# A Conformer block on one core: the fourth value product's left-over keys on all 128 rows, the last softmax sums in two bf16 halves, and the second batch's value loads three ticks apart

## The chip, the cores and the metric

The kernel runs on one core of a Trainium2 chip. The metric is the device time of one execution in microseconds; of the kernel before there are three timed runs and one profiled execution. The core has five engines with queues of their own: TensorE (PE, with its weight loads listed apart as PEld), VectorE (DVE), ScalarE (ACT), GpSimd (POOL) and SyncE (SP), which here issues nearly all transfers.

## What is computed

One Conformer block on `x` of 2 x 4000 x 512 in bf16 (D = 512, F = 2048). Cut to what matters here:

```
h  = layernorm(x);  x1 = x + 0.5 * (silu(h @ w_ff1_a) @ w_ff1_b)
h  = layernorm(x1); q, k, v = h @ w_q, h @ w_k, h @ w_v
p  = softmax(q @ k^T * D**-0.5)            # over 4000 keys, per batch
x2 = x1 + (p @ v) @ w_o
h  = layernorm(x2); a, b = split(h @ w_pw1)
dc = depthwise_conv(a * sigmoid(b), 3 taps); dc = batchnorm(dc)
x3 = x2 + silu(dc) @ w_pw2
h  = layernorm(x3); x4 = x3 + 0.5 * (silu(h @ w_ff2_a) @ w_ff2_b)
out = layernorm(x4)
```

## The kernel before, in words

**Tiling.** Tokens go in 16 chunks of up to 512 (`NCK`, eight a batch, `TCB`); the last chunk of a batch has 416. The 4000 keys of a batch make `KT` = 32 tiles of 128 rows: 31 full ones and a left-over tile with `REST` = 32 keys. Stages follow each other: first feed-forward over all chunks, attention over all chunks with the convolution of earlier chunks beside it, the rest of the convolution, second feed-forward.

**Attention.** `attention` walks over chunks `g` and, in each, over 32 ticks `kt`. Big products are done two by two blocks at a time with seven products in place of eight: keys in pairs of tiles (15 pairs), the 512 columns of the values in halves of `HD` = 256, the queries in halves of `hw` (256 columns, or 208 in the short chunk). `pv(g, n, pairs)` issues value product `n` of the seven for some pairs, each as two 128x`hw` matmuls on 128 rows of keys. Pairs come in groups `j` = 0 to 7 (`group`: pair 0, then pairs 2j-1 and 2j); `units` issues products 1, 3, 7, 5, 6 of group `j` from tick 4j+3 on. What is left of chunk `g-1` is issued in the first ticks of chunk `g` by `units_late`: `late_first`, `late_second` (with the left-over keys for products 7, 3 and 2), and `late_third` in ticks 2 to 6 (products 2 and 4 of all 15 pairs, then the left-over keys for product 4).

**Left-over keys.** Tile 30 (128 keys) and tile 31 (32 keys) have no partner and are done plainly by `pv_rest(g, tail, ns)`. For tile 31 (`tail` = 1) the probabilities lie four times in `ptail`, once in each group of 32 rows, and the 32 keys lie four times in `h[31]`; each product number in `ns` takes a row group of its own with `tile_position`. Products 7, 3 and 2 are issued together, in three row groups; product 4 alone, two matmuls on rows 0 to 31. Its values are `Vs[1]`, the difference of the two halves of `h[31]`, made by `v_rest(1)` on DVE: for batch 1 in tick 27 of chunk 0 (steps in `keys_swap`), for batch 2 in chunk 8.

**Softmax sums.** One column of the value halves is ones, so the sum of the probabilities comes out as one row of a product. `sum_row` puts it into `lrow`, one row of 512 f32 numbers. In chunks 0 to 14 it goes through memory into a column per query. After the last chunk, `attention_end` calls `sums_direct` between `late_third` for product 2 and `late_third` for product 4: four f32 matmuls of one row by one column (`lrow` times 1.0) turn the row into four columns, and a reciprocal gives `rl`. The projections of the last chunk read `rl` when they add to the residual.

**Values of batch 2.** While batch 1 is worked on, `v_ahead` makes the forms of batch 2's values and stores them. In chunk 8 `v_back(j, 0)` loads group `j` of the halves (`hv`, 256 KB a pair) and `v_back(j, 1)` the fourth form `V4`. All are issued by SP. `v_stream` loads the two other forms (`V12`, from `v12d`) per group and chunk; `key_queries` loads keys transposed.

**Order.** The calls are not the order of issue. `Plan` takes all instructions with estimated costs, keeps PE close to the order of the calls (it may issue ready work up to 8 us of estimated time early), and orders the other engines by due time. It makes six passes and takes the best by its own estimate. `Plan.cost` counts a matmul with `tile_position` at a quarter. Waits between engines are on semaphores; each engine works in its order.

All instructions pass through one helper, so the profile gives them one line; groups are told apart by the tiles: `y` and `s` are the PSUM banks, `sums`, `xt`, `keys`, `work` and `wff` the five regions of SBUF.

Of the kernel before, what the change touches and what calls it, by code (L numbers as in the profile page):

```python
# [8 lines left out]
ALU = mybir.AluOpType  # L9
# [3 lines left out]
B, T, D, F, KW = 2, 4000, 512, 2048, 3  # L13


TILE = 128
TPC = 4
CHUNK = TPC * TILE
# [11 lines left out]
HC, HD, HF = CHUNK // 2, D // 2, FC // 2  # L30
KT = -(-T // 128)
REST = T % 128
# [9 lines left out]
def width(c):  # L42

    return CHUNK if c % TCB < TCB - 1 else T - (TCB - 1) * CHUNK
# [515 lines left out]
class Conformer:  # L560
# [35 lines left out]
    def memory(self):  # L596
# [32 lines left out]
        o = oF + 2 * 6 * 2 * HC  # L629
# [16 lines left out]
        o = TCB * 4096  # L646
# [7 lines left out]
        at = [8192 + t % self.CONV_SLOTS * 4096 if t < self.NBESIDE else 20480 + (t - self.NBESIDE) * 4096  # L654
              for t in range(NCK)]
# [20 lines left out]
        C = Region(nc, "work", 48992)  # L676
        off = [0]

        def take(n):
            o = off[0]  # L680
            off[0] += n
            return o
# [18 lines left out]
        oHL = take(2048)  # L701
# [36 lines left out]
        self.zero, self.b_zero = self.P[0], self.b_P[0]  # L738
        lrow, self.b_lrow = C.view(oACC + 2048, CHUNK, F32, parts=1), C.buf("lrow", oACC + 2048, 4 * CHUNK)
        self.lrow, self.lflat = lrow.rearrange("o (p t) -> o t p", t=TPC), lrow  # L740
        self.lrowd = nc.dram_tensor("lrowd", [1, CHUNK], F32, kind="Internal").ap()
        self.b_lrowd = Buf("lrowd")
        self.u4, self.b_u4 = C.view(oACC, CHUNK, F32), C.buf("u4", oACC, 4 * CHUNK)
# [1122 lines left out]
    def pv_rest(self, g, tail, ns):  # L1866

        W, hw = width(g), width(g) // 2
        kt = KT - 1 if tail else KT - 2
        x, b_x = (self.ptail, self.b_ptail) if tail else (self.P30, self.b_P30)  # L1870
        v, b_v = self.h[kt], self.b_h[kt]
        vs, b_vs = self.Vs[tail], self.b_Vs[tail]
        forms = {3: (v[:, HD:D], b_v, 0), 7: (v[:, HD:D], b_v, 1), 2: (v[:, 0:HD], b_v, 0), 4: (vs, b_vs, 1)}
        for u in range(2):
            for j, n in enumerate(ns):
                form, b, q = forms[n]
                ps, b_ps = self.bank(self.PV_BANK[n])
                r, at = (slice(j * REST, (j + 1) * REST), {"tile_position": (j * REST, 0)}) if tail else (slice(0, 128), {})
                self.mm(ps[:, u * hw:(u + 1) * hw], form[r, u * 128:(u + 1) * 128], x[r, q * hw:(q + 1) * hw],
                        False, u == 1, [b, b_x], b_ps, skip_group_check=True, **at)  # L1880

# [56 lines left out]
                  self.v12d[b][i:i + n].rearrange("n p d -> p n d"), self.b_V12[j % 2][at:at + n], reads=self.b_v12d[b][i:i + n])  # L1938

    def v_rest(self, k):  # L1940
        x = self.h[KT - 2 + k]
        self.S.op("DVE", lambda e: e.tensor_tensor(out=self.Vs[k], in0=x[:, 0:HD], in1=x[:, HD:D], op=ALU.subtract),
                  reads=[self.b_h[KT - 2 + k]], writes=[self.b_Vs[k]])

    def v_ahead(self, i, step):
# [263 lines left out]
    def keys_swap(self, g, kt):  # L2209

        at = g * KT + kt
        if g == 0:
            steps = [(1, n) for n in range(5)] if kt == 3 else []
            j, r = divmod(kt + 1, 4)
            if 1 < j < GROUPS:
                steps += {0: [(j, 0)], 1: [(j, 1)], 2: [(j, 3)], 3: [(j, 2), (j, 4)]}[r]
            for j, n in steps:
                self.v_here(j, n)
            if kt in (26, 27):
                self.v_rest(kt - 26)  # L2220
        i, r = divmod(at - KT - 4, 10)
        if 0 <= i < PAIRS:
            for n in {0: (0,), 4: (1, 2), 5: (3, 4), 8: (5,)}.get(r, ()):
                self.v_ahead(i, n)
        if TCB - 1 <= g <= TCB:
            at -= (TCB - 1) * KT
            for k in range(KT):
                if (6 + k * (2 * KT - 12) // KT if k < KT - 1 else KT + 6) == at:
                    self.key_queries(1, k)
            for j in range(GROUPS):  # L2230
                if at == KT + 3 + j:
                    self.v_back(j, 0)
                if at == KT + 14 + j:
                    self.v_back(j, 1)
            if at in (KT + 11, KT + 12):
                self.key_values(1, KT - 2 + at - KT - 11)
            if at in (KT + 18, KT + 19):
                self.v_rest(at - KT - 18)
# [106 lines left out]
        self.residual(ps, b_ps, tile_at(g, ti), self.rl[s][r, ti:ti + 1], [self.b_rl[s]], r, total)  # L2345

    def sums_direct(self, s):
        ps, b_ps = self.sbank()
        for ti in range(TPC):
            self.mm(ps[0:TILE, ti:ti + 1], self.lrow[:, ti], self.onef[0:1], True, True,  # L2350
                    [self.b_lrow, self.b_onef], b_ps, inc=ti == TPC - 1)
        self.S.op("DVE", lambda e: e.reciprocal(self.rl[s], ps[0:TILE, 0:TPC]),
                  reads=[b_ps], writes=[self.b_rl[s]])

# [799 lines left out]
```

## Time and profile before

| what | value |
|---|---|
| median of 3 runs | 1866.38 us (1866.32 to 1868.34) |
| the profiled execution itself | 1868.96 us |
| its span, first to last instruction | 1864.0 us |
| PE busy | 1845.8 us, 99% of the span |
| DVE, ACT, POOL busy | 77%, 72%, 8% |
| granted TensorE clock, mean | 0.999 |
| moved by DMA | 228.49 MB, mean 123 GB/s |

The span is what the profile shows; the execution's own time has some 5 us more around it. Matmuls are pipelined: the next one starts before the one ahead has ended, so the time from start to start says what one costs, not its duration. In the timeline a row stands for several equal instructions: its first start, its length, their count.

### The profile page before, as it was taken

How to read it: one execution, taken by the hardware profiler on the slowest of the kernel's cores; microseconds unless marked ns; L12 is line 12 of the kernel's file. 1: busy time of each engine (PE TensorE's matmuls, PEld its weight loads, DVE VectorE, ACT ScalarE, POOL GpSimd, SP SyncE). 2: the span in 40 equal slices, each digit the busy share in tenths (PEclk: the TensorE clock that was granted, in tenths of full speed). 3: DMA queues.
4: the chain of work that ended last, by engine and by line, in shares of the span. 5: the costliest groups of instructions: out<-in, count | busy, mean ns of one | idle time of the engine just before them, and what ended most of it. 6: DMA issues, size and time to landing. Idle time of an engine off the chain costs nothing.

```text
span 1864.0 us, 39949 instructions
## 1 busy us (share of the span) xinstructions
PE 1845.8 (99%) x15838; PEld 1488.5 (80%) x15838; DVE 1428.7 (77%) x3087; ACT 1350.1 (72%) x2390; POOL 139.9 (8%) x354
## 2 busy tenths in 40 slices
PE   9999999999999999999999999999999999999998
PEld 6888888866778777887678788778875888888887
DVE  8889999868566767766765667766768888888896
ACT  6887777754656777677666767777768778778776
POOL 3000000000000000000100000000011000000000
PEclk9999999999999999999999999999999999999999
DMA  7333344297545655457944434543475222221211
GB/s 200 84 90 88 82 112 99 64 260 221 168 130 139 180 153 153 118 157 154 250 133 126 125 107 115 139 128 105 120 212 162 63 69 70 67 59 47 60 36 57
DMA packets 312520, 228.49 MB, mean 123 GB/s; under 512 B 191154, under 2 KB 283125, under 8 KB 312068
## 3 DMA queue, kind: packets, MB, share of 16 engines
q1 hardware_dynamic: 311796, 225.59, 44.9%
q8 instruction: 126, 2.06, 0.5%
q14 instruction: 70, 0.57, 0.1%
q10 hardware_dynamic: 528, 0.26, 0.0%
HBM read 128.99 MB, written 55.82 MB: 99 GB/s over the span
## 4 chain that ended last, share of the span: by engine, by line
PE 95%; DVE 2%; DMA 1%; ACT 1%; issue 0%; SPq 0%; POOL 0%; DVEq 0%; ACTq 0%
PE y L95 50%; PE s L95 45%; DVE work L95 1%; ACT work L95 0%; DMA work<-work 0%; DMA wff<-in_w_ff_a_dram 0%; DVE sums L95 0%; DMA xt<-v12d 0%; DVE xt L95 0%; DVE keys L95 0%; ACT keys L95 0%; ACT sums L95 0%; SPq L95 0%; DVE wff L95 0%; DVE s L95 0%
## 5 line engine op out<-in xcount | busy, mean ns | idle before, releaser
L95 ACT ACTIVATE sums<-s 128x512 bf16<-128x512 f32 (+4 forms) x505 | 295.3, 585 | 154.3 <-PE s L95 151.3
L95 DVE TENSOR_TENSOR sums<-sums 128x512 bf16<-128x512 bf16 (+3 forms) x528 | 202.2, 399 | 81.8 <-ACT sums L95 70.5
L95 ACT ACTIVATE keys<-s 128x512 bf16<-128x512 f32 (+3 forms) x275 | 157.0, 574 | 134.4 <-PE s L95 111.3
L95 PE MATMUL y<-work,keys 128*128 128x256 bf16 x1920 | 244.4, 273 | 0.6 <-DVE work L95 0.6
L95 PE MATMUL s<-work,keys 128*128 128x256 bf16 (+5 forms) x1456 | 225.1, 292 | 0.2 <-ACT sums L95 0.2
L95 PE MATMUL s<-sums 128*128 128x256 bf16 (+1 forms) x1428 | 212.5, 272 | 0.8 <-DVE sums L95 0.4
L95 ACT ACTIVATE work<-xt,work 128x512 bf16<-128x512 bf16 x268 | 205.2, 785 | 9.1 <-DVE work L95 7.4
L95 PE MATMUL y<-wff,keys 128*128 128x256 bf16 (+3 forms) x1592 | 209.3, 276 | 0.2 <-DVE keys L95 0.2
L95 PEld LDWEIGHTS y<-work,keys 128*128 128x128 bf16 x1920 | 187.6, 98 | 23.6 <-DVE work L95 1.2
L95 PE MATMUL y<-sums,keys 128*128 128x256 bf16 (+1 forms) x1440 | 205.3, 270 | 0.0
L95 PE MATMUL y<-work,wff 128*128 128x256 bf16 (+3 forms) x1308 | 195.2, 272 | 0.9 <-ACT keys L95 0.8
L95 DVE TENSOR_TENSOR keys<-keys 128x1024 bf16<-128x1024 bf16 (+2 forms) x262 | 170.4, 664 | 25.7 <-ACT keys L95 17.9
L95 PEld LDWEIGHTS y<-wff,keys 128*128 128x128 bf16 (+1 forms) x1592 | 151.2, 98 | 30.3 <-issue 3.3
L95 DVE BATCH_NORM_STATS2 work<-xt 128x6 f32<-128x512 bf16 x251 | 163.1, 682 | 2.5 <-DMA xt<-in_x_dram 1.8
L95 PEld LDWEIGHTS y<-sums,keys 128*128 128x128 bf16 x1440 | 137.9, 98 | 27.5 <-issue 3.5
L95 PEld LDWEIGHTS s<-work,keys 128*128 128x128 bf16 (+1 forms) x1456 | 118.5, 97 | 49.5 <-issue 2.5
L95 PEld LDWEIGHTS s<-sums 128*128 128x128 bf16 x1428 | 138.9, 98 | 23.4 <-DVE sums L95 0.7
L95 POOL TENSOR_TENSOR work<-work 128x4 f32<-128x4 f32 (+3 forms) x107 | 91.1, 854 | 769.2 <-DVE work L95 756.7
L95 PE MATMUL y<-sums,xt 128*128 128x256 bf16 (+1 forms) x960 | 145.2, 270 | 1.2 <-DMA xt<-v12d 1.1
L95 PEld LDWEIGHTS y<-work,wff 128*128 128x128 bf16 x1308 | 126.0, 98 | 18.4 <-issue 1.5
L95 PE MATMUL s<-work 128*128 128x512 bf16 (+4 forms) x545 | 131.6, 375 | 2.0 <-DVE work L95 1.7
L95 PE MATMUL s<-xt,keys 128*128 128x256 bf16 (+1 forms) x816 | 124.1, 270 | 0.0
(153 smaller groups left out, 3176.3 us busy)
## 6 DMA issues: line engine op xcount, KB each, us to landing
xt<-kfd SPq DMA_DIRECT2D x98, 384.0 KB, 3.3
xt<-v12d SPq DMA_DIRECT2D x105, 256.0 KB, 3.0
xd<-xt SPq DMA_DIRECT2D x28, 512.0 KB, 3.9
xt<-xd SPq DMA_DIRECT2D x28, 512.0 KB, 4.8
out_dram<-xt SPq DMA_DIRECT2D x14, 512.0 KB, 2.9
xt<-in_x_dram SPq DMA_DIRECT2D x13, 512.0 KB, 4.4
dcvd<-wff SPq DMA_DIRECT2D x48, 128.0 KB, 3.0
keys<-dcvd SPq DMA_DIRECT2D x12, 512.0 KB, 3.9
```

Source lines behind the costliest of these rows:

```text
L95: return getattr(eng, self.name)(*self.args, **self.kw)
```

## The change

- `pv_rest`: product 4 of tile 31 uses all 128 rows instead of rows 0 to 31. So that rows 32 to 127 add nothing, `Vs[1]` is set to zero once (POOL, tick 25 of chunk 0), and `v_rest(1)` writes rows 0 to 31 alone.
- `sums_direct`: the row of sums is split on DVE into a bf16 part and the bf16 of what is left; eight bf16 matmuls (two a column, added in PSUM) take the place of the four f32 ones.
- `keys_swap`: `v_back(j, 0)` for `j` of 2 and more is issued at ticks 6, 9, 12, 15, 18 and 21 of chunk 8 instead of 5 to 10.

```diff
+        self.lsplit = [C.view(oHL + n * 1024, CHUNK, parts=1).rearrange("o (t p) -> o t p", t=TPC) for n in range(2)]
+        self.b_lsplit = [C.buf("lsplit", oHL + n * 1024, 2 * CHUNK) for n in range(2)]
...
-                r, at = (slice(j * REST, (j + 1) * REST), {"tile_position": (j * REST, 0)}) if tail else (slice(0, 128), {})
+                r, at = (slice(j * REST, (j + 1) * REST), {"tile_position": (j * REST, 0)}) if tail and n != 4 else (slice(0, 128), {})
...
     def v_rest(self, k):
-        x = self.h[KT - 2 + k]
-        self.S.op("DVE", lambda e: e.tensor_tensor(out=self.Vs[k], in0=x[:, 0:HD], in1=x[:, HD:D], op=ALU.subtract),
+        x, r = self.h[KT - 2 + k], slice(0, REST if k else 128)
+        self.S.op("DVE", lambda e: e.tensor_tensor(out=self.Vs[k][r], in0=x[r, 0:HD], in1=x[r, HD:D], op=ALU.subtract),
...
+            if kt == 25:
+                self.S.op("POOL", lambda e: e.memset(self.Vs[1], 0.0), writes=[self.b_Vs[1]])
...
-                if at == KT + 3 + j:
+                if at == KT + 3 + (j if j < 2 else 3 * (j - 1)):
                     self.v_back(j, 0)
...
     def sums_direct(self, s):
+        (hi, lo), (b_hi, b_lo) = self.lsplit, self.b_lsplit
+        self.S.op("DVE", lambda e: e.tensor_copy(hi, self.lrow), reads=[self.b_lrow], writes=[b_hi])
+        self.S.op("DVE", lambda e: e.tensor_tensor(out=lo, in0=self.lrow, in1=hi, op=ALU.subtract),
+                  reads=[self.b_lrow, b_hi], writes=[b_lo])
         ps, b_ps = self.sbank()
         for ti in range(TPC):
-            self.mm(ps[0:TILE, ti:ti + 1], self.lrow[:, ti], self.onef[0:1], True, True,
-                    [self.b_lrow, self.b_onef], b_ps, inc=ti == TPC - 1)
+            for x, b in ((hi, b_hi), (lo, b_lo)):
+                self.mm(ps[0:TILE, ti:ti + 1], x[:, ti], self.one3[0:1, 0:1], x is hi, x is lo, [b, self.b_one3], b_ps,
+                        inc=ti == TPC - 1 and x is lo)
```

## The prediction

> **What bounds the kernel now.** I read the page first, then the stretches by chunk, then the waits of TensorE, then the timeline of each place that the change touches.
>
> ```profile
> span 1864.0 us, 39949 instructions
> PE 1845.8 (99%) x15838; PEld 1488.5 (80%) x15838; DVE 1428.7 (77%) x3087; ACT 1350.1 (72%) x2390; POOL 139.9 (8%) x354
> PE 95%; DVE 2%; DMA 1%; ACT 1%; issue 0%; SPq 0%; POOL 0%; DVEq 0%; ACTq 0%
> ```
>
> TensorE is busy 99% of the span and carries 95% of the chain that ended last. So time is won in two ways only: TensorE issues less or issues closer together, or one of its few waits goes. Work on the other engines and transfers cost nothing until TensorE waits for them. By chunk (the stretches: us, busy us of PE, PEld, DVE, ACT, POOL, granted clock, DMA share, GB/s), chunk 7 and then chunk 8, in which the moved loads are:
>
> ```profile
> 828.00:884.00 56.00, 54.81 (x532) 46.09 (x530) 37.41 (x88) 42.48 (x86) 3.15 (x13) 1.00 0.74 157
> 884.00:952.00 68.00, 67.80 (x499) 44.28 (x497) 46.60 (x117) 44.00 (x79) 5.59 (x21) 1.00 0.90 227
> ```
>
> All that TensorE waits for from the end of chunk 0 to the end of attention (461 to 1376 us; total, times, longest):
>
> ```profile
> PE y L95 <- DMA xt<-v12d: 1.1, 1, 1.1
> PE s L95 <- ACT sums L95: 1.0, 2, 0.8
> PE s L95 <- ACT s L95: 0.3, 1, 0.3
> PE s L95 <- DVE xt L95: 0.2, 1, 0.2
> ```
>
> These 2.6 us in 915 are all that a new order of the other engines can give back there. The busy time hides something else: products on 32 rows.
>
> **Fourth value product (pv_rest, late_third).** One chunk's left-over keys in the timeline of PE (start, us, what):
>
> ```profile
> 475.76 0.38 PE L95 MATMUL y<-sums,work 128*128 128x256 bf16 x2
> 475.98 0.38 PE L95 MATMUL y<-xt,sums 128*128 128x256 bf16 x2
> 476.30 0.39 PE L95 MATMUL y<-wff,sums 32*128 32x256 bf16 x2
> 476.62 0.39 PE L95 MATMUL y<-sums,keys 128*128 128x256 bf16 x2
> ```
>
> Two products on 128 rows take 0.22 us from start to start (475.76 to 475.98). Going into the pair on 32 rows takes 0.32 (475.98 to 476.30), coming out of it 0.32 again: 0.10 lost on each side, 0.20 a chunk. The products themselves are no shorter for having 32 rows: 273 ns each in the group below. On 128 rows the pair is like its neighbours and both losses go. The group (count, busy us, mean ns of one) has all of these pairs, two products a chunk in 14 chunks of 256 columns:
>
> ```profile
> L95 PE MATMUL y<-wff,sums 32*128 32x256 bf16 x28 | 5.4, 273 | 0.0
> ```
>
> In the two short chunks (208 columns) the last one, with the sums ahead of it, reads:
>
> ```profile
> 1376.24 2.85 PE L95 MATMUL y<-sums,keys 128*128 128x208 bf16 x30
> 1379.06 2.02 PE L95 MATMUL s<-work 1*128 1x1 f32 x8
> 1381.01 2.85 PE L95 MATMUL y<-sums,work 128*128 128x208 bf16 x30
> 1383.70 0.34 PE L95 MATMUL y<-xt,sums 128*128 128x208 bf16 x2
> 1383.97 0.35 PE L95 MATMUL y<-wff,sums 32*128 32x208 bf16 x2
> 1384.25 1.90 PE L95 MATMUL s<-work,wff 128*128 128x512 bf16 x8
> ```
>
> Thirty products from 1381.01 to 1383.70 are 0.090 each, 0.18 a pair; the steps around the 32-row pair are 0.27 and 0.28, so 0.19 is lost. Sum: 16 x 0.20 = **3.2 us gained**. The six 32-row products of 7, 3 and 2 keep their mode change. Bounds: 3.0 to 3.2, since in the built order of the changed kernel all 16 pairs stand between 128-row products.
>
> The Trainium skill, page TensorEngine Tiling (Array Packing), section Theoretical Speedup, speaks against this edit: a contraction of 32 or less should run up to four times as fast in tiles. Here two products in one tile have no neighbour tile to run beside, and the rows above decide against the rule; its result is a rival below.
>
> What the edit adds beside: one memset of 128x256 on POOL, once in chunk 0, and a subtraction on 32 rows in place of 128. POOL is busy 8%, and this row is the nearest:
>
> ```profile
> L95 POOL MEMSET work<- 1x512 f32 x1 | 0.5, 514 | 3.3 <-DVE xt L95 3.3
> ```
>
> It stands two ticks ahead of the subtraction that writes after it, so half a microsecond hides there: 0 (if that cover were gone, at most its 0.5).
>
> **Last softmax sums (sums_direct).** Four f32 products run as eight passes. The thirty before them end their issue at 1376.24 + 30 x 0.090 = 1378.93; the next product starts at 1381.01: 2.08 us for the sums. For the eight bf16 products of one row the nearest is the transpose of the taps, four products of three rows:
>
> ```profile
> 61.59 0.82 PE L95 MATMUL y<-work,keys 128*128 128x256 bf16 x6
> 62.34 0.25 PE L95 MATMUL y<-work 3*128 3x3 bf16 x4
> 62.52 0.50 PE L95 MATMUL s<-sums 128*128 128x256 bf16 x3
> ```
>
> Six products of 0.109 end their issue at 62.24, and the next wide one starts at 62.52: 0.28 for four with the change of mode both ways. Four more at some 0.03 make 0.40. So 2.08 - 0.40 = 1.7 is gained on TensorE. Against it stand two DVE operations that the products now wait for, a cast and a subtraction over 512 elements of one row. DVE at this place, and the nearest prices by form:
>
> ```profile
> 1378.30 0.70 DVE L95 TENSOR_TENSOR work<-s,work 1x128 f32<-1x128 f32 x2
> 1381.12 0.18 DVE L95 RECIPROCAL work<-s 128x4 f32<-128x4 f32 x1 [1.84 <-PE s L95]
> 1387.12 1.54 DVE L95 SCALAR_TENSOR_TENSOR xt<-s,work,xt 128x512 bf16<-128x512 f32 x2 [0.66 <-PE s L95]
> L95 DVE CAST xt<-s 128x512 bf16<-128x512 f32 x2 | 1.3, 668 | 0.0
> L95 DVE TENSOR_TENSOR work<-y,sums 128x512 f32<-128x512 f32 x14 | 9.6, 689 | 0.5 <-DVE sums L95 0.2
> ```
>
> The last row sum ends at 1379.00; cast and subtraction, one needing the other, end near 1379.00 + 0.67 + 0.69 + 0.1 = 1380.5. In the built order 14 of the 30 following products now stand ahead of the sums: TensorE gets there at 1378.93 + 14 x 0.090 = 1380.19 and waits some 0.3. Behind the waiting product are 16 products of the same chunk and all projections. I take 1.7 - 0.4 = **1.3 us gained**; 1.7 without a wait, 0.7 if the two operations take half as long again. The reciprocal that follows has 6 us of cover: its first reader starts at 1387.12. The Trainium skill, page VectorE: DVE Perf Modes, section The perf-mode tier table, puts an f32 copy within SBUF at twice the rate of one from PSUM, which my cast row is; by that this term would be 1.6. No row here shows it, and the source is read with a stride.
>
> **Value loads of batch 2 (v_back).** Groups 2 to 7 load at ticks 6, 9, ... 21 of chunk 8 in place of 5, 6, ... 10. Before, on SP:
>
> ```profile
> 888.07 1.57 SPq L95 DMA_DIRECT2D keys<-vhd  x3
> 894.09 6.72 SPq L95 DMA_TRANSPOSE work<-keysd  x1
> keys<-vhd SPq DMA_DIRECT2D x7, 512.0 KB, 5.8
> ```
>
> Chunk 8 is where DMA is busiest (0.90), but TensorE is busy 67.80 of 68.00 there, so spreading has 0.2 us to win. It costs nothing either while the loads come in time: a tick is 68.0/32 = 2.1 us, group j is first used at tick 4j+3, so group 2 still has 5 ticks, 10.6 us, against 5.8 to land; later groups have more. **0**, from -0.2 to 0.3.
>
> **The new order.** The planner reorders everything from chunk 1 to the end of attention. The one DMA wait of chunk 7 is a value form that left SP late:
>
> ```profile
> 857.56 0.32 SPq L95 DMA_DIRECT2D xd<-xt  x1
> 865.24 0.58 SPq L95 DMA_DIRECT2D xt<-v12d  x1
> 867.10 1.26 SPq L95 DMA_TRANSPOSE work<-work  x1
> 869.03 1.20 SPq L95 DMA_TRANSPOSE work<-work  x1
> 870.27 0.58 SPq L95 DMA_DIRECT2D xt<-v12d  x1
> 875.94 0.44 PE L95 MATMUL y<-sums,xt 128*128 128x208 bf16 x3 [1.09 <-DMA xt<-v12d]
> ```
>
> Counted from the same `xd<-xt`, the changed order puts that load ahead of these two transposes and behind one more store, about 2 us sooner: the 1.1 us wait should go (0 to 1.1). Against it ACT has two new runs of four tap scalings ahead of score copies. The known run of four in chunk 15 stays:
>
> ```profile
> 1357.62 2.92 ACT L95 ACTIVATE work<-xt,work 128x512 bf16<-128x512 bf16 x4
> ```
>
> It ends in the 0.8 and 0.3 us waits for ACT above; runs of three, six of them, cost next to nothing. For the two new ones I take 0.3 each, between 0 and 1.1. Net **0.5 us gained**, between 1.1 gained and 2.2 lost.
>
> **Sum.** 3.2 + 1.3 + 0 + 0.5 = 5.0 us. The profiled execution itself took 1868.96 us, so its like would take 1863.96; it ran 2.58 above the median of the runs, 1866.38, from which the forecast is 1866.38 - 5.0 = **1861.4**.
>
> **Rivals.**
> - Only the mode changes count: the sums wait for DVE as long as they save, or the new runs on ACT eat the rest. For it: the sum clears 0.2% (3.7 us, about what a measurement of this kernel can tell from no change) by 1.3 only, and 3.2 alone doesn't. Against it: 1.7 us less issue at the end has few ways to be eaten whole. 1866.38 - 3.2 = 1863.2, the same within 0.2%.
> - Slower: the value loads of chunk 8 come late. Group 2's margin is 10.6 - 5.8 = 4.8 us, and SP is held 6.72 us by one transpose at 894.09. From 5 us of delay on, each microsecond more is an idle one on TensorE, in up to six groups; at 1.5 each, 9 us, 1866.38 + 9 - 4.5 = 1870.9. Against it: the built order puts the loads of groups 0 to 3 ahead of that transpose, and the others have over 12 us.
> - The tile rule: a 32-row pair costs a quarter, 0.05 us, and the change adds 0.17 a chunk, 2.7 in all: 1866.38 + 2.7 - 1.8 = 1867.3, the same. Against it: every 32-row row above.
>
> **How the numbers follow.** The forecast has a chance of 0.68, the first rival 0.25, the slow one 0.05, the tile rule 0.02. The range: best case 3.2 + 1.7 + 1.1 + 0.2 = 6.2, and a microsecond for a median of few runs (they span 2.0), gives 1859.2; at the other end 3.0 + 0.7 - 2.2 = 1.5, 1864.9, which holds the first rival. Faster 0.68, same 0.27, slower 0.05.
>
> **What would show it.** In the changed profile: no `y<-wff,sums` on 32 rows, and steps of 0.22 or 0.18 where they were; the sums in less than 0.8 us, wait included; no wait for `xt<-v12d` in chunk 7; none for `keys<-vhd` in chunk 8; waits for ACT between 461 and 1376 us below 2 us. I am wrong if the steps around the fourth product stay at 0.32, or if new waits of over 2 us stand in that stretch.

## The result, and the profile after

| kernel | median of its runs | lowest to highest | profiled execution, its span |
|---|---|---|---|
| before (6 runs beside the changed one) | 1867.45 us | 1866.32 to 1868.68 | 1868.96 us, 1864.0 |
| changed (6 runs) | 1860.28 us | 1859.74 to 1861.06 | 1859.74 us, 1854.8 |

The ratio is 0.9962 with a 95% interval from 0.9949 to 0.9975: 7 us faster, where 5.0 was forecast (1861.4, from 1859.2 to 1864.9). The page of the changed kernel, its span, the busy time of each engine and the shares of the chain that ended last:

```profile
span 1854.8 us, 39946 instructions
PE 1840.5 (99%) x15838; PEld 1490.4 (80%) x15838; DVE 1429.7 (77%) x3090; ACT 1349.4 (73%) x2388; POOL 140.5 (8%) x356
PE 96%; DVE 2%; ACT 1%; DMA 0%; issue 0%; SPq 0%; DVEq 0%
```

TensorE's count has not moved, since eight bf16 products stand for eight f32 passes. Its busy time fell by 5.3 us, and the DMA's 1% of the chain is gone. The stretches of chunks 7 and 8, cut where each chunk's first product on row groups starts (columns as in the prediction):

```profile
826.59:880.80 54.21, 54.21 (x531) 46.46 (x530) 34.86 (x81) 41.18 (x83) 3.46 (x13) 1.00 0.70 152
880.80:948.69 67.89, 67.69 (x498) 44.44 (x498) 47.51 (x121) 44.37 (x80) 4.30 (x21) 1.00 0.89 233
```

Chunk 7 has no idle time left (54.21 busy of 54.21; before, 54.81 of 56.00). Chunk 8 has what it had. All that TensorE waits for from 461 to 1376 us:

```profile
PE s L95 <- ACT sums L95: 0.9, 2, 0.7
PE s L95 <- DVE work L95: 0.4, 1, 0.4
PE s L95 <- ACT s L95: 0.3, 1, 0.3
```

The `xt<-v12d` wait and the one for DVE's `xt` are gone, a wait for DVE's `work` (the split of the sums) has come. No row names `keys<-vhd`. The left-over keys of the same chunk as before:

```profile
475.27 0.38 PE L95 MATMUL y<-xt,sums 128*128 128x256 bf16 x2
475.49 0.38 PE L95 MATMUL y<-wff,sums 128*128 128x256 bf16 x2
475.71 0.38 PE L95 MATMUL y<-sums,keys 128*128 128x256 bf16 x2
475.93 0.38 PE L95 MATMUL s<-sums,keys 128*128 128x256 bf16 x2
```

Every pair starts 0.22 us after the one ahead; the 0.32 on both sides of the 32-row pair are gone. And the sums, PE first, then DVE:

```profile
1372.80 1.41 PE L95 MATMUL y<-sums,work 128*128 128x208 bf16 x14
1374.15 0.17 PE L95 MATMUL s<-work 1*128 1x1 bf16 x1
1374.69 0.32 PE L95 MATMUL s<-work 1*128 1x1 bf16 x7 [0.37 <-DVE work L95]
1374.95 1.60 PE L95 MATMUL y<-sums,work 128*128 128x208 bf16 x16
```

```profile
1372.17 0.71 DVE L95 TENSOR_TENSOR work<-s,work 1x128 f32<-1x128 f32 x2
1372.91 0.62 DVE L95 CAST work<-work 1x512 bf16<-1x512 f32 x1
1373.57 1.07 DVE L95 TENSOR_TENSOR work<-work 1x512 bf16<-1x512 f32 x1
1375.05 0.18 DVE L95 RECIPROCAL work<-s 128x4 f32<-128x4 f32 x1
```

Fourteen products of 0.0893 end their issue at 1374.05; the next wide one starts at 1374.95. So the sums cost 0.9 us in place of 2.08, 0.37 of it a wait for the subtraction. The first product, on the high half, did not wait for it.

To place the rest, the traces of all kernels but e9, which has no such row groups, are cut at the same products: chunks 1 to 15, then from the last chunk's first product on row groups to the first projection (the sums lie here), then to the third group of 160 columns in the last chunk's product with `w_pw1`. All in us:

| kernel | chunks 1 to 15 | end of attention | projections, to the last `w_pw1` product | span |
|---|---|---|---|---|
| before | 914.68 | 8.29 | 16.40 | 1864.0 |
| before again (e4) | 914.46 | 8.29 | 16.40 | 1861.4 |
| rows, old order (e2) | 911.15 | 8.10 | 16.39 | 1859.9 |
| order alone (e3) | 912.37 | 8.29 | 15.85 | 1861.4 |
| rows and order (e1) | 909.29 | 8.10 | 15.91 | 1857.3 |
| sums alone (e5) | 914.08 | 7.10 | 16.40 | 1861.2 |
| loads alone (e6) | 914.47 | 8.29 | 16.40 | 1864.1 |
| all but the loads (e7) | 910.40 | 6.91 | 15.91 | 1856.7 |
| changed | 909.27 | 6.91 | 15.91 | 1854.8 |
| changed again (e8) | 909.25 | 6.89 | 15.91 | 1855.7 |
| changed, third time (e11) | 909.29 | 6.88 | 15.91 | 1855.6 |
| changed, sums later (e10) | 909.28 | 6.38 | 15.85 | 1855.2 |

From before to changed these three columns lose 5.41 + 1.38 + 0.49 = 7.3 us (7.1 from the second execution of before), which is the whole change of the medians. Some of the 0.49 does not last: to the four 128x128 products at 1415.17 us before and 1407.38 after, counted from the first projection, it is 30.92 against 30.64, so 0.28. What the span varies beyond the three columns (1854.8 against 1855.7 for one program) lies ahead of chunk 1 and behind them, and comes and goes with the execution. Single chunks repeat to 0.02 us from one execution of a program to the next, but for chunks 7 and 8 of those kernels that wait for a transfer there. That is why differences far below the scatter of the whole time can be read here.

### The profile page after: what moved, and what is told of

The parts are those of the page before. It is cut to its first block, busy times and chain, and to the rows that moved or that the text cites. A ratio compares the mean times of both kernels' runs of the same rounds, so it can differ in the third digit from the quotient of the medians.

```text
span 1854.8 us, 39946 instructions
## 1 busy us (share of the span) xinstructions
PE 1840.5 (99%) x15838; PEld 1490.4 (80%) x15838; DVE 1429.7 (77%) x3090; ACT 1349.4 (73%) x2388; POOL 140.5 (8%) x356
## 4 chain that ended last, share of the span: by engine, by line
PE 96%; DVE 2%; ACT 1%; DMA 0%; issue 0%; SPq 0%; DVEq 0%
PE y L95 50%; PE s L95 46%; DVE work L95 1%; ACT work L95 1%; ACT keys L95 0%; DMA xt<-in_x_dram 0%; DMA work<-work 0%; ACT sums L95 0%; DVE wff L95 0%; ACT wff L95 0%; DVE xt L95 0%; DVE sums L95 0%; DVE keys L95 0%; DVE s L95 0%; ACT s L95 0%
## 5 line engine op out<-in xcount | busy, mean ns | idle before, releaser
L95 DVE TENSOR_TENSOR s<-s,xt 128x512 f32<-128x512 f32 (+1 forms) x98 | 67.6, 690 | 94.7 <-PE s L95 65.3
```

The lines of the kernel that those rows point to most:

```text
L95: return getattr(eng, self.name)(*self.args, **self.kw)
```

## The experiments

My theory was that of the prediction: mode changes, then sums, then the planner's order, and nothing for the loads. The rivals: only the mode changes count; the order does it; the loads do it. Dots in the code stand for lines that are not shown. Edits e1 to e6 are shown against the kernel before, e7, e9 and e10 against the changed one. The median of before was 1866.83 us beside e1 to e4 (33 runs), 1867.53 beside e5 to e8 (26 runs) and 1867.04 beside e9 to e11 (15 runs).

**e1: the fourth value product alone.**

```diff
-                r, at = (slice(j * REST, (j + 1) * REST), {"tile_position": (j * REST, 0)}) if tail else (slice(0, 128), {})
+                r, at = (slice(j * REST, (j + 1) * REST), {"tile_position": (j * REST, 0)}) if tail and n != 4 else (slice(0, 128), {})
...
+            if kt == 25:
+                self.S.op("POOL", lambda e: e.memset(self.Vs[1], 0.0), writes=[self.b_Vs[1]])
```

> The fourth product on 128 rows alone; sums and value loads as before. Its order of issue on all engines is that of the changed kernel up to chunk 8. Theory (mode and order): the mode change of the array gives 16 x 0.20 = 3.2 us, and the new order that the planner made of it gives about 2 more (the wait for a value form in chunk 7, 1.1 to 1.6, and small ones): 5.2 to 5.5 below before, no wait for xt<-v12d in chunk 7. Rival (mode alone, the rest of the change gave the rest): 3.2 below.

Measured: 1863.46 us, ratio 0.9983 (0.9974 to 0.9992). By its time that is 3.4 below before, as the rival had it, and not 5.2 to 5.5. In the stretches of its trace it gains more than the 3.3 us of mode changes: 5.39 + 0.19 + 0.49 = 6.1 against before; why the time shows less comes under e3 and e8. The chunks are those of the changed kernel, and TensorE's order of issue is the same but for the sums. So this edit, and not the sums or the loads, carries the new order: the planner counts a matmul with `tile_position` at a quarter, and the pair now has its full cost.

**e2: the same edit, but the planner goes on costing the pair at a quarter,** so that its order stays the old one.

```diff
-            return (n / 2.4 + 2.5) * (0.25 if at is not None else 1)
+            return (n / 2.4 + 2.5) * (0.25 if at is not None or self.quarter else 1)
...
+                if self.S.plan:
+                    self.S.plan.quarter = bool(tail and n == 4)
```

> The fourth product on 128 rows, but the planner still counts the pair at a quarter, so that the order of issue on every engine stays that of before. Mode and order: 3.2 us below before, steps of 0.22 us around the pair in all chunks, and the wait for xt<-v12d of about 1.1 us stays in chunk 7. Rival (the time is won by the 128-row pair itself, wait included): 5 below, and the wait is gone.

Measured: 1864.59 us, 0.9986 (0.9977 to 0.9995), so 2.2 below before, between 0.9 and 4.3; the trace tells more. Its rows at the left-over keys, and what TensorE waits for from 461 to 1376 us:

```profile
475.32 0.38 PE L95 MATMUL y<-xt,sums 128*128 128x256 bf16 x2
475.54 0.38 PE L95 MATMUL y<-wff,sums 128*128 128x256 bf16 x2
475.76 0.38 PE L95 MATMUL y<-sums,keys 128*128 128x256 bf16 x2
```

```profile
PE s L95 <- ACT sums L95: 1.0, 2, 0.8
PE y L95 <- DMA xt<-v12d: 0.6, 1, 0.6
PE s L95 <- ACT s L95: 0.3, 1, 0.3
PE s L95 <- DVE xt L95: 0.2, 1, 0.2
```

Steps of 0.22, with all the old waits in place: the mode changes by themselves.

**e3: the order alone.** The pair stays on 32 rows, and the planner is told its full cost.

```diff
-            return (n / 2.4 + 2.5) * (0.25 if at is not None else 1)
+            return (n / 2.4 + 2.5) * (0.25 if at is not None and not self.full else 1)
...
+                if self.S.plan:
+                    self.S.plan.full = bool(tail and n == 4)
```

> The fourth product stays on 32 rows, but the planner counts the pair in full: the order of issue is that of e1, the mode change is kept. Mode and order: 1.6 to 2.3 us below before, no wait in chunk 7, steps of 0.32 us around the pair. Rival (mode alone): the same as before within 0.5. Rival (tile rule): as the rule has the pair at a quarter, e1 is slower than this one by 2.7.

Measured: 1866.38 us, 0.9997 (0.9988 to 1.0006), the same by its time, as the first rival had it. In the stretches, though, it gains 2.1 in the chunks and 0.55 behind them against e4. Its steps and waits:

```profile
475.42 0.38 PE L95 MATMUL y<-xt,sums 128*128 128x256 bf16 x2
475.73 0.39 PE L95 MATMUL y<-wff,sums 32*128 32x256 bf16 x2
476.05 0.39 PE L95 MATMUL y<-sums,keys 128*128 128x256 bf16 x2
```

```profile
PE s L95 <- ACT sums L95: 0.9, 2, 0.7
PE s L95 <- ACT s L95: 0.3, 1, 0.3
```

Steps of 0.31 and 0.32 stay, two waits are gone. The four kernels close: e3 to e1 is 3.08 + 0.19 = 3.3 us for the mode changes in 16 chunks (0.205 each; e4 to e2 gives 3.5, with a shorter DMA wait in it), and e4 to e3 or e2 to e1 is 2.6 or 2.3 for the order. Why the order does not show in e3's time: the median span of its runs is 1.6 below that of the runs beside it (1860.4 against 1862.0), but the execution lasts 6.07 us longer than its span in the median of e3's runs, against 4.93 for e4. (The difference between 1.6 and the 2.6 of the traces is not placed.) The same 6 us stand in e1 (5.95) and e7 (5.95), and 4.8 to 5.3 in all the others, the changed kernel among them (5.11). The three are the kernels that have the new order with the old loads. What lies outside the span the profile doesn't show; this stays open.

**e4: the kernel before once more.** No edit.

> The kernel before once more, nothing changed. It tells what two profiles of one program differ by: in the first stage and in the second feed-forward, where the changed program has the same order, its profile was 0.7 and some 1.5 us shorter than that of before. If that is from execution to execution, this span lies 1 to 2.5 us below 1864.0 and the time is the same within 0.1%. If the first profile was typical, the span is 1864 and these 2.2 us are a gain that I have not explained.

Measured: 1867.29 us, 1.0002 (0.9993 to 1.0011). The span is 1861.4: the 2.6 us more of the first trace came with that execution. The wait for `xt<-v12d` in chunk 7 was 0.8 us here, 1.1 in the first trace, 0.6 in e2, 0.5 in e5, and none is listed in e6, all with the old order. It is a transfer, and varies with the execution.

**e5: the sums alone.**

```diff
...
-            self.mm(ps[0:TILE, ti:ti + 1], self.lrow[:, ti], self.onef[0:1], True, True,
-                    [self.b_lrow, self.b_onef], b_ps, inc=ti == TPC - 1)
+            for x, b in ((hi, b_hi), (lo, b_lo)):
+                self.mm(ps[0:TILE, ti:ti + 1], x[:, ti], self.one3[0:1, 0:1], x is hi, x is lo, [b, self.b_one3], b_ps,
+                        inc=ti == TPC - 1 and x is lo)
```

> The two bf16 halves of the last sums alone; the fourth product and the value loads as before, order of issue as before up to the end of attention. In the changed profile the sums hold TensorE for 0.98 us from the last product ahead to the next one, before for 2.17. Theory (parts add up): the same 1.2 us here, all chunks as in e4 to 0.01 us, 1.2 below before. Rival (the second product's wait for DVE is longer when the array isn't ahead): the sums at 1.5 or more, 0.5 below before.

Measured: 1866.12 us, 0.9995 (0.9986 to 1.0004); too little for the time to tell. The end of attention shows it: 8.29 to 7.10, 1.19 us, and e1 to changed is 8.10 to 6.91, again 1.19.

**e6: the loads alone.**

```diff
-                if at == KT + 3 + j:
+                if at == KT + 3 + (j if j < 2 else 3 * (j - 1)):
```

> The value loads of batch 2 three ticks apart, nothing else. Theory (off the path): TensorE waits for no transfer in chunk 8 before or after; chunk 8 stays at 68.09 us, time the same within 0.5. Rival (contention): DMA is busy 0.90 in chunk 8, and thinning it speeds the transposes that chunks 8 and 9 wait for: chunk 8 or 9 shorter by 0.3 to 1. Rival (late loads): a wait for keys<-vhd appears in chunk 8 or 9.

Measured: 1867.51 us, 1.0000 (0.9991 to 1.0009). With the old order the loads win nothing by the time. In the trace chunk 8 was 0.69 longer than in e5, by a wait for DVE that no other trace has, and chunk 7 was shorter:

```profile
903.54 0.83 PE L95 MATMUL y<-sums,keys 128*128 128x256 bf16 x6 [0.51 <-DVE wff L95]
```

What held DVE up is a change of order: in e6 the planner puts the reciprocal of an earlier chunk's sums ahead of two scalings, and TensorE waits for the second of them. The reciprocal waits 0.89 us for its transfer (`work<-lrowd`) and starts at 901.66; the second scaling runs from 902.79 to 903.48, and TensorE starts at 903.54. In the kernel before, the reciprocal stands behind those scalings (904.88, they start at 902.48 and 903.20). So e6 is not the loads alone. But the traces of before, e4 and e5 list no wait for a transfer in chunk 8 that the loads could take away.

**e7: the changed kernel with the loads at their old ticks.**

```diff
-                if at == KT + 3 + (j if j < 2 else 3 * (j - 1)):
+                if at == KT + 3 + j:
```

> The changed kernel with the value loads back at ticks 5 to 10. The order of issue on PE and ACT is that of the changed kernel to the last instruction. Theory (off the path): same time as the changed kernel within 0.7 and the same length of every chunk to 0.1. Rival (the loads are what brings the changed kernel below the sum of e1 and e5): 1.5 to 2 above the changed kernel, with the loss in chunk 8 or 9.

Measured: 1862.25 us, 0.9973 (0.9964 to 0.9983); e8, the changed kernel on the same chip, 1860.76. So my theory, no change, failed here, and the rival, 1.5 to 2 above with the loss in chunk 8 or 9, came: 1.5 above. In the medians 0.85 of it lies in the span (1856.3 against 1855.45) and 0.62 outside (5.95 against 5.33). In the traces all chunks are those of the changed kernel but chunk 8: 69.03 in place of 67.88. The place in e7, then in the changed kernel, PE's timeline:

```profile
917.23 1.03 PE L95 MATMUL s<-work,keys 128*128 128x512 bf16 x4
919.23 0.61 PE L95 MATMUL y<-sums,xt 128*128 128x256 bf16 x4 [0.98 <-DMA xt<-v12d]
```

```profile
917.68 0.59 PE L95 MATMUL s<-work,keys 128*128 128x512 bf16 x2
918.11 0.60 PE L95 MATMUL y<-sums,xt 128*128 128x256 bf16 x4
```

The wait is for a streamed value form that stands on SP behind the loads and transposes. Its issue in e7, in the changed kernel, and in e1, which has the old loads too and did not wait (SP's timeline, three kernels):

```profile
913.13 0.59 SPq L95 DMA_DIRECT2D xt<-v12d  x1
```

```profile
911.34 0.53 SPq L95 DMA_DIRECT2D xt<-v12d  x1
```

```profile
911.35 0.58 SPq L95 DMA_DIRECT2D xt<-v12d  x1
```

Chunk 8 starts at 880.8 in all three. So the old loads leave this transfer at the edge: 1.8 us later in e7 than in e1, where it was in time, with one order on SP. What held SP up in e7 is not known. With the new loads chunk 8 was 67.88 in all four executions traced with this order (changed, e8, e10, e11). That the loads take away a wait that sometimes comes is what these few traces suggest; how often it comes they can't say.

**e8: the changed kernel once more,** and e11, the same again beside e9 and e10.

> The changed kernel again, on the same chip and beside the same runs of before as e5 to e7. If parts add up, its distance to before is e1 (3.4 in the medians) plus e5 (1.2) plus e6 (0): 4.6 to 5, and the 7.2 of the first comparison had 2 from the execution. If it is 7 again, the parts help each other or the rest of the program differs between the two.

> The changed kernel once more, on the same chip as the two kernels beside it: 1860.4 us, span 1855, chunk lengths equal to those of its other executions to 0.05 us but for chunk 7 and the second feed-forward.

Measured: 1860.76 us, 0.9966 (0.9953 to 0.9978), and 1860.92, 0.9965 (0.9952 to 0.9979). The chunks repeat to 0.02 us. The times of the parts do not add up: e1, e5 and e6 lie 3.4, 1.4 and 0.0 below before, 4.8 in all, and the whole change 6.8. Of the 2.0 that are missing, 1.15 lie in the spans (medians: 4.5 + 1.3 + 0.1 against 7.05) and 0.8 outside them. e7 points at the reason: the old loads cost 1.5 us in the new order, and e1 has that order with the old loads. Whether executions of e1 other than the traced one wait in chunk 8 was not seen.

**e9: products 7, 3 and 2 on all 128 rows too.**

```diff
-                r, at = (slice(j * REST, (j + 1) * REST), {"tile_position": (j * REST, 0)}) if tail and n != 4 else (slice(0, 128), {})
+                r, at = (slice(j * REST, (j + 1) * REST), {"tile_position": (j * REST, 0)}) if False else (slice(0, 128), {})
```

> The changed kernel with the left-over keys of products 7, 3 and 2 on all 128 rows as well (their 32 keys lie four times in that tile, so they count four times there). This asks whether row groups pay where three stand side by side. In the changed kernel the six products of a chunk take 0.29 us from the first start to the next wide product in the short chunk and 0.09 more to get in (1369.65 to 1369.83 to 1370.12), 0.42 in a chunk of 256 columns. My theory (a pass costs its columns, three row groups share one, a change of mode costs 0.1 on each side): six products of 0.109 are 0.65, so each long chunk is 0.23 longer and each short one 0.16, 3.5 us in all, less or more by what the planner's order does: 1863.8 us, slower than the changed kernel and still faster than the one before. Rival (row groups never pay beside the changes of mode): the six products take no longer than 0.42 on 128 rows and the time is that of the changed kernel within 0.5.

Measured: 1864.83 us, 0.9990 (0.9981 to 0.9999): 3.9 above the changed kernel beside it, where my theory had 3.5 and the rival at most 0.5. The six products in the last chunk's late work, in the changed kernel and in e9:

```profile
1369.65 0.25 PE L95 MATMUL y<-xt,keys 128*128 128x208 bf16 x1
1369.83 0.26 PE L95 MATMUL y<-wff,keys 32*128 32x208 bf16 x1
...
1369.94 0.25 PE L95 MATMUL y<-wff,keys 32*128 32x208 bf16 x1
1370.12 2.85 PE L95 MATMUL y<-sums,keys 128*128 128x208 bf16 x30
```

```profile
1372.14 0.25 PE L95 MATMUL y<-xt,keys 128*128 128x208 bf16 x1
1372.23 0.25 PE L95 MATMUL y<-wff,keys 128*128 128x208 bf16 x1
...
1372.67 0.25 PE L95 MATMUL y<-wff,keys 128*128 128x208 bf16 x1
1372.76 2.84 PE L95 MATMUL y<-sums,keys 128*128 128x208 bf16 x30
```

From the last wide product ahead to the first one behind it is 0.47 on row groups (1369.65 to 1370.12) and 0.62 on 128 rows. So three row groups side by side do pay, even with a change of mode on each side: two passes of 0.09 stand for six. The pair of product 4 had no neighbour and took two full passes. Part of the 3.9 is the planner again: in e9 the split of the sums comes later, and TensorE waits 0.90 us for it in place of 0.37.

**e10: the sums behind the last products of product 4.**

```diff
         self.late_third(o, 2, range(PAIRS))
-        self.sums_direct(o % TCB % 2)
         self.tick()
         self.late_third(o, 4, range(PAIRS))
+        self.sums_direct(o % TCB % 2)
```

> The changed kernel with sums_direct called after the last products of product 4 in place of ahead of them, so that TensorE has 18 products of 0.089 us more to do while DVE splits the row. My theory: the 0.37 us wait for the subtraction goes, the eight products with their changes of mode stay at 0.5, the reciprocal comes 1.6 later and still ahead of its first reader: 0.4 us less from the last chunk's end to the first projection (6.5 in place of 6.9), too little for the time (1860.3). Rival: the reciprocal becomes late for the first residual and through it for TensorE; then the stretch behind it is longer by what was won.

Measured: 1859.83 us, 0.9961 (0.9947 to 0.9975), 1.1 below e11 beside it, less than a measurement can tell. The end of attention does tell: 6.38 in place of 6.88 to 6.91.

```profile
1375.29 0.34 PE L95 MATMUL y<-wff,sums 128*128 128x208 bf16 x2
1375.56 0.35 PE L95 MATMUL s<-work 1*128 1x1 bf16 x8
1375.85 1.04 PE L95 MATMUL s<-work,wff 128*128 128x512 bf16 x4
```

The wait is gone, and the eight products with both changes of mode cost 1375.85 - 1375.29 - 2 x 0.09 = 0.38. The stretch behind is no longer (15.85), so the reciprocal is still in time. The gain is 0.5 where the wait that went read 0.37.

That is no accident: a stop of TensorE costs more than its listed idle time. Chunk 7 of the kernel before:

```profile
874.32 0.53 PE L95 MATMUL y<-sums,keys 128*128 128x208 bf16 x4
875.94 0.53 PE L95 MATMUL y<-sums,xt 128*128 128x208 bf16 x4 [1.09 <-DMA xt<-v12d]
```

Four products of 0.089 end their issue at 874.68 and the next starts 1.26 later, with 1.09 listed. In e7 it is 917.23 + 4 x 0.215 = 918.09 to 919.23, 1.14, with 0.98 listed; the 0.37 at the sums cost 0.5. Each time some 0.16 comes on top: the listed idle time counts from the end that the profile gives the last product (it is modelled), 0.25 us behind its start, while the next could have started after 0.09.

## Why the prediction was right, and where not

**Fourth value product: 3.2 forecast, 3.3 measured** (e3 to e1; e2). The step was right in mechanism and size. The tile rule of the Trainium skill (TensorEngine Tiling (Array Packing), section Theoretical Speedup) as a rival falls: a pair on 32 rows alone cost two full passes and two changes of mode. Where row groups do stand side by side the rule's direction agrees with e9.

**Sums: 1.3 forecast, 1.19 measured** (e5). The parts were off in two directions. The products with their changes of mode took 0.38, against 0.40 forecast. The cast took 0.62 against 0.67, the subtraction 1.07 against 0.69. TensorE's wait reads 0.37 where 0.4 was taken, and cost 0.5. That the term came out near is in part luck: the subtraction took half as long again as forecast, and the change of mode on the way in and the first product, 0.12 us, fit into the time that DVE still needed. With 0.9 us, wait included, the sums also miss the "less than 0.8" named as a sign; the other signs came as named. The cast gives no support to a copy within SBUF at twice the rate (VectorE: DVE Perf Modes, The perf-mode tier table, in the Trainium skill): 0.617 us on one row with a stride, against 0.668 from PSUM on 128 rows.

**Loads: 0 forecast, from -0.2 to 0.3.** In the old order the time says the same (e6, 1.0000), with DVE's order changed beside. In the new order it was too narrow: without the moved loads the median is 1.5 us higher (e7 against e8), and of the traced executions one took 1.15 us longer in chunk 8 (e7), another not (e1). The step that failed is "TensorE is busy 67.80 of 68.00 there, so spreading has 0.2 us to win": it read the old order's chunk, and did not ask how near to late the streamed values come when the order changes. The rival of late value loads did not happen; the transfer that did come late was `xt<-v12d`, and with the old loads, not the new.

**The new order: 0.5 forecast, 2.3 to 2.9 measured** at the cuts of the table (0.2 less some 30 us behind the first projection), beyond my bound of 1.1. This term was mis-sized, and in the traces it makes up the difference between 5.0 and 7.2. In the times of all runs the loads have a share in it, by e7 up to 1.5, and the runs do not part the two further. Chunk 7 lost 1.81 us, 0.21 of it by the mode change, so 1.6 for a wait that the list gave as 1.1: 0.16 for the stop, and the rest in stops that the list leaves out. Such a one is here, before:

```profile
844.55 0.60 PE L95 MATMUL y<-work 128*128 128x256 bf16 x4
845.25 0.34 PE L95 MATMUL y<-sums,xt 128*128 128x208 bf16 x2
```

Four products of 0.109 end their issue at 844.99 and the next starts at 845.25: 0.26 lost, with no wait shown. e6 bears it out: no wait is listed in its chunk 7, and with 54.98 us the chunk is still 0.56 longer than in e3, which has the new order. Chunk 15 lost 0.65, 0.2 by the mode change: the DVE wait went and the longer ACT wait shrank from 0.8 to 0.7. And the waits of the convolution's rest, which my list from 461 to 1376 did not reach (1384 to 1401 us, before):

```profile
PE y L95 <- DVE work L95: 0.4, 1, 0.4
PE y L95 <- ACT keys L95: 0.2, 1, 0.2
```

Neither is listed in that stretch of the changed kernel, which is 0.5 shorter at the cut of the table and 0.28 some 30 us behind the first projection. The cost that I set against it, 0.3 for each new run of four scalings on ACT, did not come: the ACT waits are what they were.

So "2.6 us in 915 are all that a new order can give back there" was wrong as a working: the listed waits that went are 1.4 us (1.1, 0.2 and 0.1 of the first trace), and 2.1 to 2.3 us came back there (e3 against e4 and before). It added up listed waits, and neither the stops' own cost nor the stretch behind. The forecast came out because the large term was read from starts and not from durations, and the error in the order lay on the gaining side. That the time lies inside the range is in part luck: the gain of 7.2 is above the best case of 6.2, and the range held it because it starts from 1866.38, the median of three runs, 1.1 below that of the six runs of before beside the changed kernel, and allows a microsecond for scatter. (Its other end, 1.5, leaves out the 0.3 that the loads could cost.) The first rival (only the mode changes count, 1863.2) describes e2 but not the change.

## What to carry to other kernels

When TensorE is the bound, price an edit by the distance from start to start in the timeline, on both sides of the place: here a narrow product cost its columns and its changes of mode, whatever its rows, so that a row group paid only with neighbours. Where a planner costs instructions, an edit that alters an instruction's estimated cost is also a change of order everywhere, and the two can be told apart by holding the estimate or the instruction fixed (e2 and e3). For what a wait may give back, measure from the last start to the next start: the listed idle time was 0.16 us too small for each stop.

## What the runs showed of the hardware

- A change between 128-row products and products on fewer rows cost about 0.1 us each way; the whole of it, 0.205 us a chunk, came back when the rows were made equal (e3 to e1).
- A stop of TensorE cost its listed idle time and some 0.16 us more: 1.26 for 1.09 in chunk 7, 1.14 for 0.98 in chunk 8 of e7, 0.5 for 0.37 at the sums.
- The DVE subtraction of 1x512 from f32 into bf16 took 1.05 to 1.07 us in every trace, longer than the 0.69 of a 128x512 one that reads PSUM, though it has one row. Why was not tried; its source has a stride.
- Executions of e1, e3 and e7 took 5.95 to 6.07 us beyond their span in the median, those of the other kernels 4.8 to 5.3. No run of the three lies below 5.76 and none of the others above 5.58; no trace shows the cause.
